# Attention and a gated MLP on one core: a byte-wise step in the weight conversion, and a new order of all operations

## The chip, the cores and the metric

One core of one Trainium2 chip. The metric is device time of one launch in microseconds (us), median of the runs. The five engines that matter are TensorE (PE, matmuls; PEld are its weight loads), VectorE (DVE), ScalarE (ACT), GpSimd (POOL) and SyncE (SP), which issues every DMA of this kernel, one after the other.

## The reference, cut to what matters

```
q, k, v: [4, 8, 768, 64] float32          w_in: [512, 2048], w_out: [2048, 512] float64
k_sum, v_sum = max of k, mean of v over blocks of 32 keys           # 24 each
scores  = [q k^T / 8 where |i - j| < 16,   q k_sum^T / 8 + log 32]
x       = softmax(scores) @ [v, v_sum]     # gathered to [3072, 512]
h       = x @ w_in
out     = (h * cos(h)) @ w_out             # [3072, 512] float32
```

## The kernel before, in words

**Attention.** The 3072 rows of x are eight blocks (0 to 7) of 384 rows, half a batch each. A block has four groups a, b, c, d of two heads. In the tables of the order `a0` is group a of block 0. A group loads q, k and v (`q`, `k`, `v`; 192 KB, 384 KB and about 280 KB by the shapes) and the sums of v (`m`, two DMAs, 72 KB), turns q and k so that the head dimension lies on the partitions (`tq`, `tk` on PE, or `qt`, `kt` on DVE), places them, takes block maxima of k (`ks`), writes the mask into PSUM (`ms`, first eight groups), multiplies (`sc`), copies the scores out (`z`), then maximum (`mx`, DVE), subtraction (`su`, POOL), exponential (`ex`, ACT), sum and inverse (`sm`, `iv`, DVE), normalization (`nm`, POOL), transposition (`tp` on PE with copies `cp`, or `pt`, `po`, `pi`: a 32x32 transpose on DVE and a way through DRAM), the product with v (`va`, PE), and the high and low part of x (`xh`, `xl`).

**Sums of v.** `v0_0` and `v0_1` are the two sums of batch 0 (768 KB each; `l` load, `h` halve, `s` sum). Every later batch has eight parts (`v1_0` to `v1_7`, 192 KB), which share one tile, `kn`: the load of a part waits until the part before is summed.

**Weights.** The float64 weights come as pairs of 32-bit words in 16 slices (`w0` to `w15`, 1 MB each, of a [512, 128] piece of w_in and a [128, 512] piece of w_out). For each slice: `l` load (two DMAs); `ab` (ACT, line 380) takes the absolute value of the high words, 128x1024; `cl` (line 385) clamps them; `sh` (DVE, line 391) shifts left by 3 and masks; `lb` (DVE, line 399) ors in the top three bits of the low words; `fb` (DVE, line 407) ors in the sign and top exponent bit; `hi` and `lo` split the float32 into two fp32r parts. A slice lands in one of six tiles `late`, which are reused: the load of `w5` waits for `fb` of `w1`, `w4` for `w0`, `w8` for `w2`, `w9` for `w3`, `w6` for `w4`.

**MLP.** A step `s` is a block of rows and one slice. `up` (PE, line 706) is 12 matmuls of 384 columns into one PSUM bank; `tu`, `si` (ACT), `re`, `ga` (DVE) make h cos h; `hi`, `lo` split it; `dh` and `dl` (PE, line 757) are 6 and 3 matmuls of 512 columns into three PSUM banks that stay open for the whole run. Steps 0 to 5 are block 0 with slices 0 to 5, steps 6 to 21 block 1 with all slices, steps 22 to 31 block 0 with slices 6 to 15, and then 16 steps for each block. `st` stores a result. Step 0 needs x of all four groups of block 0; step 6 needs all of block 1; step 12 is the first that needs slice 6, step 20 the one for slice 14.

**The order.** `ORDER` is a text of 2118 tokens such as `s4.up.5` (object, operation, PSUM bank or buffer, engine `a`, `v` or `p`). The program walks through it and emits each operation; on every engine the instructions run in just this order, SP's DMAs too, and an instruction that waits holds back all that stand behind it on its engine. The framework adds the semaphores.

Of the kernel before, what the change touches and what calls it, by code (L numbers as in the profile page):

```python
# [32 lines left out]
d0.sc w1.lb a0.nm c0.ex a0.v d0.z.1.a w1.fb.1 a0.tp.0.3 d0.z.0.a a0.tp.1.0 w0.ab.0 a0.m d0.mx w1.hi.a w0.cl.v d0.su
d0.m c0.sm w0.sh.4.5 w5.l w1.lo.p c0.iv w2.ab.0 w0.lb c1.m a0.cp.0.a w2.cl.v c0.nm d0.ex b1.q w0.fb.1 a0.cp.1.a w3.l
a0.va.1 d0.sm w0.hi.a d1.m w2.sh.6.7 w0.lo.p c0.tp.0.2 c1.q d0.iv w5.ab.0 w2.lb b1.tq.3 a1.q a0.xh.a d0.nm c0.tp.1.0
w2.fb.1 c0.cp.0.a d0.v c0.cp.1.a w5.cl.v w2.hi.a c0.va.2 a0.xl w2.lo.p d0.tp.0.6 c0.xh.a w5.sh.4.5 w4.l d0.tp.1.7 a1.m
b0.mx w3.ab.0 a1.tq.0 w5.lb b0.su a1.v a1.cq.a a1.ms.1.0 w5.fb.1 w3.cl.p b0.ex b0.m d0.cp.0.a a1.sc b0.sm b1.cq.a
c1.tq.6 d0.cp.1.a c0.xl a1.z.1.a d0.va.3 b0.iv w3.sh.4.5 b0.nm a1.z.0.a b1.m c1.ms.7.2 d0.xh.a a1.mx c1.cq.a d1.q
w4.ab.0 c1.sc w3.lb a1.su b0.v b0.tp.0.0 w5.hi.a b0.tp.1.1 d0.xl w4.cl.v c1.z.0.a c1.v b0.cp.0.a w4.sh.6.7 c1.z.1.a
b1.ms.3.0 b0.cp.1.a v1_0.l c1.mx a1.ex w8.l w4.lb c1.su b0.va.2 b1.sc a1.sm b0.xh.a w5.lo.p c1.ex d1.tq.1 b0.xl  # L40
b1.z.1.a a2.q a1.iv s0.up.2 w4.fb.0 b1.z.0.a a1.nm w3.fb.1 w4.hi.a a1.tp.0.0 d1.cq.a w4.lo.v w9.l d1.ms.3.6 s0.tu
a1.cp.0.a b1.v c1.sm w8.ab.0 a1.tp.1.7 d1.sc s0.re c1.iv a1.cp.1.a s1.up.4 w8.cl.v c1.nm w10.l s0.si b1.mx d1.v
w8.sh.0.1 w3.hi.a b1.su a1.va.5 d1.z.0.v s1.tu c1.tp.0.7 w8.lb w3.lo.p a2.v d1.z.1.a c1.tp.1.3 a2.tq.6 s1.re c1.cp.1.a
a1.xh.a s2.up.3 d1.mx s1.si c1.cp.0.a s0.ga d1.su w7.l w8.fb.0 s0.hi.a c1.va.2 s0.lo.p w9.ab.1 s1.ga w6.l s3.up.7
w8.hi.v s2.tu b2.q s1.hi.v d1.ex w9.cl.v s1.lo.p a1.xl s0.dh.0.1.4 s2.re w8.lo.p c1.xh.v s3.tu s0.dl c1.xl s2.si s3.re
s4.up.5 a2.cq.v v1_0.s.p d1.sm s3.si s2.ga s1.dh w7.ab.0 d1.iv s2.hi.v d1.nm v1_1.l w9.sh.2.3 s1.dl b1.ex s3.ga
s2.lo.p d1.tp.0.6 w9.lb d1.tp.1.7 s2.dh w7.cl.p s4.tu b1.sm d1.cp.1.a s2.dl d1.cp.0.a s4.re b1.iv s3.hi.a d1.va.7
w9.fb.1 b1.nm s4.si s5.up.6 w7.sh.2.3 s3.lo.p w9.hi.v d1.xh.a s3.dh s4.ga s5.tu w9.lo.p w10.ab.0 d1.xl s5.re s3.dl
w7.lb s4.hi.a b1.tp.0.5 s5.si v1_1.s.p b1.tp.1.7 s4.dh b1.cp.1.a w7.fb.1 b1.cp.0.a s5.ga w7.hi.a b1.va.7 v1_2.l
s4.lo.v w10.cl.v s4.dl s5.hi.a w7.lo.p b1.xh.a s5.dh b1.xl w10.sh.2.3 s6.up.5 v1_2.s.p w6.ab.1 w10.lb s7.up.6 w10.fb.0  # L50
s6.tu s5.lo.p v1_3.l s6.re w12.l w6.cl.v s6.si s5.dl s7.tu w10.hi.v s8.up.7 s7.re w10.lo.p s5.ta.2.a s6.ga s7.si
v1_3.s.v s9.up.2 s5.ta.1.a s7.ga v1_4.l s6.hi.a w6.sh.4.5 s5.st.2 s5.ta.0.a s6.lo.p b2.m s7.hi.a s10.up.3 s8.tu w6.lb
s7.lo.p w12.ab.0 s8.re v1_4.s.p s11.up.6 w6.fb.1 s8.si s9.tu s8.ga v1_5.l w6.hi.a w12.cl.v s6.dh.4.5.7 w11.l s9.re
w6.lo.p w12.sh.0.1 s9.si a2.m s6.dl s8.hi.a s7.dh s5.st.1 s9.ga s8.lo.p s5.st.0 w12.lb s7.dl s8.dh v1_5.s.p s10.tu
s9.hi.a s10.re w12.fb.1 s10.si s8.dl s12.up.2 v1_6.l w11.ab.0 s9.lo.v w15.l s10.ga w12.hi.a w11.cl.v s13.up.3
w11.sh.0.1 s11.tu w12.lo.p s10.hi.a s11.re s9.dh w11.lb s11.si s10.lo.p s11.ga s9.dl w11.fb.1 v1_6.s.p s12.tu s10.dh
w15.ab.0 s12.re w13.l s14.up.6 s11.hi.a w15.cl.v s12.si v1_7.l s11.lo.v b2.v s13.tu s12.ga s10.dl s13.re s12.hi.a
s11.dh w15.sh.0.1 w11.hi.a s12.lo.p w11.lo.p s11.dl s14.tu w15.lb s13.si s12.dh w13.ab.0 s14.re s12.dl v1_7.s.p
w15.fb.1 s15.up.2 s14.si s13.ga s13.hi.a s14.ga a2.k w13.cl.v s13.lo.p s16.up.3 s14.hi.a w15.hi.a w13.sh.0.1 w15.lo.p
s15.tu w13.lb s17.up.6 s15.re w13.fb.0 s15.si s14.lo.p s13.dh s16.tu w14.l s13.dl s16.re s15.ga a2.tk.0.0 s16.si  # L60
a2.tk.1.1 s15.hi.v s14.dh a2.ks.0 s15.lo.p b2.k a2.ck.1.a a2.ks.1 a2.ck.0.a s16.ga s17.tu a2.sc.2.1 w13.hi.a s17.re
s18.up.0 a2.z.1.v w13.lo.p a2.z.0.v b2.qt w14.ab.1 a2.mx s14.dl s17.si w14.cl.v a2.su s15.dh s16.hi.a w14.sh.2.3
s15.dl s17.ga s16.lo.p a2.ex s16.dh w14.lb s16.dl w14.fb.0 s18.tu s19.up.1 s17.hi.a a2.sm w14.hi.a s17.lo.p a2.iv
s18.re s17.dh a2.nm b2.kt.0 s18.si b2.kt.1 w14.lo.p s17.dl b2.ks.0 c2.k a2.tp.0.6 b2.ks.1 b2.sc.2.3 a2.cp.0.a s18.ga
s19.tu a2.tp.1.0 c2.q s20.up.6 b2.z.0.v a2.cp.1.a b2.z.1.v s18.hi.v s19.re s18.lo.p s19.si s21.up.2 s20.tu s20.re
b2.mx s20.si s22.up.0 s19.ga b2.su c2.kt.0 s19.hi.v b2.ex s23.up.3 c2.kt.1 s19.lo.p c2.ks.1 d2.k b2.sm s18.dh s21.tu
s21.re b2.iv s18.dl s21.si c2.qt s19.dh c2.ks.0 d2.q s20.ga s20.hi.v c2.sc.1.6 s20.lo.p s21.ga a2.va.2 s22.tu s21.hi.a
s19.dl d2.kt.0 c2.v s22.re s20.dh s21.lo.p c2.z.0.v a2.xh.v b2.nm s23.tu s20.dl d2.kt.1 s22.si d2.ks.1 s21.dh d2.qt
s23.re a3.q s21.dl s22.ga s23.si s24.up.1 d2.ks.0 s21.ta.1.1.a c2.z.1.v s22.hi.v s21.ta.2.0.v s22.lo.p b2.tp.0.0 c2.mx
b2.tp.1.5 d2.sc.6.7 b2.cp.1.a b2.cp.0.v c2.su s24.tu a2.xl b2.va.5 s24.re s25.up.0 d2.z.0.v b2.xh.a d2.m a3.qt s24.si  # L70
b2.xl c2.ex s21.st.1 d2.z.1.v s26.up.2 c2.m s23.ga s23.hi.v d2.mx s23.lo.p s21.st.2 c2.sm s27.up.6 v2_0.l d2.su s25.tu
c2.iv s24.ga c2.nm s25.re s22.dh.5.7.3 s25.si s22.dl s24.hi.v c2.pt.1 s23.dh s24.lo.p s21.ta.0.0.v c2.po b3.q s26.tu
# [872 lines left out]
```

## Time and profile before

| | |
|---|---|
| median of 3 runs | 661.79 us (661.63 to 662.5) |
| the profiled execution | 663.55 us, of which the span of the profile is 661.8 us |
| busy: PE, DVE, ACT, POOL | 96%, 68%, 46%, 33% of the span |
| chain that ended last, by engine | PE 86%, DMA 4%, SP queue 3%, DVE 3%, POOL 2%, ACT 1% |
| DMA | 72.67 MB, mean 110 GB/s |

Busy PE says little alone, because matmuls are pipelined; the table by stage in the prediction, with idle time, granted clock (PEclk, 1.00 is full speed) and DMA share of each stretch, is the one to read. A row of the timeline has start, duration, engine, line, operation, and in brackets how long the engine sat idle before it and what ended that.

### The profile page before, as it was taken

The numbers are of one execution on the slowest core, as the hardware profiler recorded it, in microseconds if no ns is written. First come the engines' busy times: TensorE is split into PE (matmuls) and PEld (weight loads), VectorE is DVE, ScalarE is ACT, GpSimd is POOL, SyncE is SP. The second block draws the span as 40 slices with busy tenths as digits, with TensorE's granted clock in tenths as the row PEclk, the third lists the DMA queues.
The fourth block names the chain that finished last, engine by engine and source line by source line (L and its number), as shares of the span: only waits on it lengthen the run. The fifth ranks groups of instructions, "written<-read, shape, count | busy, mean of one in ns | idle before, by whom it ended". The sixth has DMA issues, their size and how long they took to land.

```text
span 661.8 us, 13155 instructions
## 1 busy us (share of the span) xinstructions
PE 633.2 (96%) x5141; PEld 560.9 (85%) x5141; DVE 449.9 (68%) x798; ACT 305.8 (46%) x512; POOL 220.7 (33%) x219
## 2 busy tenths in 40 slices
...
GB/s 222 257 271 188 289 16 215 173 113 63 59 125 82 93 120 122 139 58 113 109 104 137 137 96 106 116 43 85 108 169 101 93 94 76 0 1 17 16 17 48
DMA packets 167158, 72.67 MB, mean 110 GB/s; under 512 B 136825, under 2 KB 155833, under 8 KB 167097
## 3 DMA queue, kind: packets, MB, share of 16 engines
...
## 4 chain that ended last, share of the span: by engine, by line
PE 86%; DMA 4%; SPq 3%; DVE 3%; POOL 2%; ACT 1%; issue 1%; DVEq 0%; POOLq 0%; ACTq 0%
PE banks L757 39%; PE banks L706 39%; PE banks L561 4%; PE banks L662 3%; DMA late<-in_moe_w_out_dram 2%; SPq L448 2%; DMA late<-in_moe_w_in_dram 1%; DMA late<-in_q_dram 1%; DVE banks L391 1%; DVE stage L407 1%; POOL stage L385 1%; ACT stage L380 1%; SPq L477 0%; PE banks L548 0%; DVE banks L399 0%
## 5 line engine op out<-in xcount | busy, mean ns | idle before, releaser
L706 PE MATMUL banks<-xh,w 128*128 128x384 f32 x1024 | 272.1, 337 | 0.2 <-ACT pt L342 0.2
L757 PE MATMUL banks<-w,gh 128*128 128x512 f32 x768 | 198.1, 393 | 0.0
L706 PEld LDWEIGHTS banks<-xh,w 128*128 128x128 f32 x1024 | 185.9, 188 | 2.9 <-ACT pt L342 0.4
L706 PE MATMUL banks<-xl,w 128*128 128x384 f32 x512 | 171.4, 335 | 0.0
L757 PEld LDWEIGHTS banks<-w,gh 128*128 128x128 f32 x768 | 142.6, 188 | 28.8 <-ACT gh L342 0.3
L716 ACT ACTIVATE t<-banks 128x384 int32<-128x384 f32 x128 | 62.5, 489 | 164.8 <-DVE gl L348 60.2
L348 POOL TENSOR_TENSOR gl<-t,gh 128x384 fp32r<-128x384 f32 x55 | 56.4, 1026 | 224.0 <-PE banks L757 108.3
L719 DVE SCALAR_TENSOR_TENSOR t<-t,banks 128x384 f32<-128x384 int32 x128 | 69.9, 548 | 67.3 <-ACT t L716 66.4
L757 PE MATMUL banks<-w,gl 128*128 128x512 f32 x384 | 109.8, 394 | 1.0 <-DVE gl L348 1.0
L724 ACT ACTIVATE t<-t 128x384 f32<-128x384 f32 x128 | 66.5, 524 | 75.5 <-DVE t L719 75.1
L706 PEld LDWEIGHTS banks<-xl,w 128*128 128x128 f32 x512 | 96.1, 188 | 1.6
L757 PEld LDWEIGHTS banks<-w,gl 128*128 128x128 f32 x384 | 71.1, 188 | 15.5 <-DVE gl L348 1.1
L585 POOL TENSOR_TENSOR sc<-sc,m 128x720 f32<-128x720 f32 x28 | 40.1, 1431 | 130.3 <-DVE m L580 130.3
L728 DVE TENSOR_TENSOR t<-t,banks 128x384 f32<-128x384 f32 x128 | 69.1, 544 | 13.4 <-ACT t L724 12.4
L609 POOL TENSOR_TENSOR sc<-sc,r 128x720 f32<-128x720 f32 x28 | 39.9, 1426 | 48.9 <-DVE r L606 45.6
L342 ACT CAST gh<-t 128x384 fp32r<-128x384 f32 x68 | 34.7, 511 | 43.9 <-DVE t L728 22.4
L348 DVE TENSOR_TENSOR gl<-t,gh 128x384 fp32r<-128x384 f32 x73 | 41.5, 569 | 18.0 <-PE banks L757 9.8
L344 DVE CAST gh<-t 128x384 fp32r<-128x384 f32 x60 | 23.1, 384 | 28.6 <-PE banks L757 26.8
L348 POOL TENSOR_TENSOR w<-stage,w 128x1024 fp32r<-128x1024 f32 x15 | 36.3, 2418 | 10.4 <-ACT w L342 8.5
L572 DVE SCALAR_TENSOR_TENSOR sc<-banks,mask 128x360 f32<-128x360 f32 x48 | 24.4, 524 | 21.2 <-PE banks L561 21.2
L561 PEld LDWEIGHTS banks<-kd,qd 64*64 64x64 f32 x1344 | 28.4, 135 | 9.2 <-issue 6.6
L662 PEld LDWEIGHTS banks<-pt,vn 120*64 120x64 f32 x624 | 21.0, 141 | 13.0 <-ACT pt L342 7.0
(101 smaller groups left out, 602.1 us busy)
## 6 DMA issues: line engine op xcount, KB each, us to landing
...
```

The lines of the kernel that those rows point to most:

```text
L342: eng.copy(out=out, in_=in_)
L348: eng.tensor_tensor(out=lo, in0=src, in1=hi.bitcast(F32), op=ALU.subtract)
L561: nc.tensor.matmul(out=self.sp[hh][s * QT : (s + 1) * QT, c, lo : lo + n], lhsT=self.qd[rows, t * QT : (t + 1) * QT], rhs=self.kd[rows, ke ...
L585: nc.gpsimd.tensor_tensor(out=self.sc, in0=self.sc, in1=self.m.unsqueeze(2).broadcast_to([P, U, NK]), op=ALU.subtract)
L609: nc.gpsimd.tensor_tensor(out=self.sc, in0=self.sc, in1=self.r.unsqueeze(2).broadcast_to([P, U, NK]), op=ALU.mult)
L662: nc.tensor.matmul(out=self.xps[rows, t * QT : (t + 1) * QT], lhsT=self.vn[:, t, rows], rhs=self.pt[2 * c + hh][s], start=True, stop=True,)
L706: nc.tensor.matmul(out=self.h, lhsT=w_of(name, self.f)[:, c * P : (c + 1) * P], rhs=x_of(self.blk, part, c), start=n == 0, stop=n == last,)
L716: nc.scalar.activation(out=self.t.bitcast(I32), in_=self.h, func=AF.Copy, scale=1.0 / TWO_PI, bias=0.25)
L719: nc.vector.scalar_tensor_tensor(out=self.t, in0=self.t.bitcast(I32), scalar=-TWO_PI, in1=self.h, op0=ALU.mult, op1=ALU.add)
L724: nc.scalar.activation(out=self.t, in_=self.t, func=AF.Sin, scale=-1.0, bias=-0.5 * math.pi)
L728: nc.vector.tensor_tensor(out=self.t, in0=self.t, in1=self.h, op=ALU.mult)
L757: nc.tensor.matmul(out=self.acc[i], lhsT=g[:, i * P : (i + 1) * P], rhs=w_of(name, self.f), start=self.first and n == 0, stop=self.last an ...
```

## The change

**The weight conversion.** `ab` also multiplies by 2^-48 (an argument of the same instruction), and the clamp's bounds are multiplied likewise. `sh` is no longer a shift on DVE: it is an ACT instruction that reads byte 3 of each low word (unsigned 8-bit, every eighth byte), computes byte/32 - 15.5/32 and writes it as an integer, that is, the top three bits of the low word. It depends on the loaded words alone. `lb` now shifts the clamped words left by 3 and ors in these bits, in one DVE instruction; `fb` keeps the sign bit only. DVE has three instructions for a slice instead of four, ACT two instead of one.

```
-    W_LO = struct.unpack("f", struct.pack("I", 896 << 20))[0]
-    W_HI = struct.unpack("f", struct.pack("I", (1151 << 20) - 1))[0]
+    DOWN = 2.0 ** -48
+    W_LO = struct.unpack("f", struct.pack("I", 896 << 20))[0] * DOWN
+    W_HI = struct.unpack("f", struct.pack("I", (1151 << 20) - 1))[0] * DOWN
...
-            nc.scalar.activation(out=self.u.bitcast(F32), in_=self.high.bitcast(F32), func=AF.Abs)
+            nc.scalar.activation(out=self.u.bitcast(F32), in_=self.high.bitcast(F32), func=AF.Abs, scale=DOWN)
...
-        def shift(self, *where):
-            to = self.work_in(where)
-            nc.vector.tensor_scalar(
-                out=to, in0=self.u, scalar1=3, scalar2=0x3FFFFFFF,
-                op0=ALU.logical_shift_left, op1=ALU.bitwise_and,
-            )
-            self.u = to
+        def top_bits(self, *where):
+            self.top = self.work_in(where)
+            byte = self.raw.bitcast(U8).rearrange("p (n b) -> p n b", b=8)[:, :, 3]
+            nc.scalar.activation(out=self.top, in_=byte, func=AF.Copy, scale=1.0 / 32, bias=-15.5 / 32)
...
         def last_bits(self, *where):
-            to = self.work_in(where)
+            to = self.work_in(where) if where else self.top
             nc.vector.scalar_tensor_tensor(
-                out=to, in0=self.low, scalar=29, in1=self.u,
-                op0=ALU.logical_shift_right, op1=ALU.bitwise_or,
+                out=to, in0=self.u, scalar=3, in1=self.top,
+                op0=ALU.logical_shift_left, op1=ALU.bitwise_or,
             )
...
-                out=to, in0=self.high, scalar=-(1 << 30), in1=self.u,
+                out=to, in0=self.high, scalar=-(1 << 31), in1=self.u,
```

**The order.** All of `ORDER` is replaced; the set of operations is the same 2118. PE's matmuls are the same in number and shape. Their order, the PSUM banks, the order of the DMAs and the engine of some operations differ:

| operation | before | after |
|---|---|---|
| low part of a step's product (`lo`) | POOL 55, DVE 73 | POOL 69, DVE 59 |
| parts of the sums of v (`s`) | POOL 12, DVE 14 | POOL 17, DVE 9 |
| clamp of a slice (`cl`) | POOL 2, DVE 14 | POOL 3 (w7, w6, w14), DVE 13 |
| copies out of PSUM (`z`, `ck`, `cq`, `xh`) | ACT 48, DVE 67 | ACT 41, DVE 74 |
| negated results (`ta`) | ACT 14, DVE 10 | ACT 12, DVE 12 |

SP's order up to what step 0 waits for, before and after (`l`, `q`, `k`, `v`, `m` are loads):

```
before: b0.k a0.q a0.k c0.q c0.k d0.k v0_1.l v0_0.l b0.q w1.l d0.q w0.l c0.v c0.m w2.l a0.v a0.m d0.m w5.l c1.m b1.q
        w3.l d1.m c1.q a1.q d0.v w4.l a1.m a1.v b0.m b1.m d1.q b0.v c1.v v1_0.l w8.l a2.q w9.l b1.v w10.l d1.v a2.v
        w7.l w6.l b2.q v1_1.l v1_2.l v1_3.l w12.l
after:  a0.k a0.q d0.k c0.k b0.k b0.q v0_1.l c0.q v0_0.l c0.v w1.l d0.q a0.v w0.l c0.m w2.l a0.m b1.q w5.l d0.m c1.q
        w3.l a1.q d0.v w4.l b0.v d1.q b0.m a1.v w8.l a1.m a2.q w7.l c1.m b1.v c1.v d1.v w9.l b1.m d1.m v1_0.l w10.l
        v1_1.l a2.v w6.l v1_2.l w12.l v1_3.l
```

PE's order around the first steps:

```
before: a0.tp a0.va c0.tp b1.tq c0.tp c0.va d0.tp a1.tq a1.ms a1.sc c1.tq d0.va c1.ms c1.sc b0.tp b1.ms b0.va b1.sc
        d1.tq s0.up a1.tp d1.ms a1.tp d1.sc s1.up a1.va c1.tp a2.tq s2.up c1.va s3.up s0.dh s0.dl s4.up s1.dh
after:  a0.tp c0.tp a0.va c0.va a1.ms b1.tq d0.tp c1.tq a1.tq a1.sc d0.va c1.ms c1.sc b0.tp b1.ms b0.tp b1.sc d1.tq
        b0.va d1.ms d1.sc s0.up s1.up s2.up a1.tp s4.up c1.tp a1.va c1.tp s3.up s0.dh s0.dl s1.dh s1.dl d1.tp
```

PE's order at step 12, after the change: `s6.up s4.dl s7.up s5.dh s5.dl s8.up s6.dh s6.dl s9.up s7.dh s7.dl s10.up s11.up s8.dh s8.dl s9.dh s9.dl s12.up`.

More of the change, by code (lines that the diff above doesn't have):

```diff
@@ L33 @@
[L33 to L72, printed above, removed]
@@ new lines @@
+w9.ab.1 w9.cl.v s2.dh s4.hi.v b1.nm b1.tp.0.0 s2.dl w9.sh.3.4 b1.tp.1.5 d1.m d1.va.7 b1.cp.1.a b1.cp.0.a d1.xh.a s3.dh
+w9.lb w9.fb.1 d1.xl w9.hi.a w7.cl.p v1_0.l v1_0.s.p s5.up.0 a2.tq.7 a2.cq.v w7.sh.3.4 w7.lb b1.va.5 s3.lo.p s4.lo.p
+b1.xh.a s5.tu s3.dl s4.dh b1.xl s6.up.5 s5.re w9.lo.p w7.fb.1 w10.l w10.ab.0 s5.si s5.ga v1_1.l a2.v w6.l v1_1.s.p
+v1_2.l v1_2.s.p w10.cl.v w7.hi.a s5.hi.v s6.tu s6.re s6.si w10.sh.3.4 w7.lo.v s5.lo.v s6.ga w10.lb w10.fb.0 s4.dl
+s7.up.0 s5.dh s5.dl s5.ta.2.v s7.tu s6.hi.a w6.ab.1 s7.re s5.ta.0.a s7.si s8.up.7 s6.lo.p w10.hi.a s5.ta.1.v s7.ga
```

240 lines of the change are left out of this document (138 added, 102 removed).

## The prediction

> **What bounds the kernel now.** I read first the table of windows by stage, for where PE stands still and at what clock.
>
> ```profile
> 0.00:16.50 16.50, 10.85 (x134) 8.32 (x134) 8.27 (x18) 5.41 (x10) 8.24 (x36) 1.00 0.94 222
> 16.50:33.00 16.50, 6.37 (x116) 4.51 (x116) 14.03 (x16) 8.70 (x15) 10.52 (x10) 0.92 0.88 257
> 33.00:50.00 17.00, 12.22 (x119) 9.10 (x120) 14.33 (x17) 9.41 (x16) 14.35 (x8) 0.50 0.93 267
> 50.00:66.00 16.00, 14.31 (x235) 10.79 (x236) 12.60 (x16) 11.40 (x21) 7.22 (x5) 0.97 0.69 188
> 66.00:100.00 34.00, 32.71 (x248) 28.21 (x248) 32.57 (x46) 25.92 (x41) 29.64 (x26) 1.00 0.52 150
> 100.00:150.00 50.00, 50.00 (x300) 45.42 (x300) 44.45 (x62) 31.64 (x53) 34.07 (x34) 1.00 0.54 166
> ...
> 650.00:661.80 11.80, 6.77 (x30) 5.26 (x28) 3.88 (x8) 1.42 (x3) 1.01 (x1) 1.00 0.18 67
> sum 661.80, PE 633.22 PEld 560.95 DVE 449.86 ACT 305.83 POOL 220.68; mean PE 37.25 PEld 33.00 DVE 26.46 ACT 17.99 POOL 12.98
> ```
>
> The columns are stretch, length, busy time of PE, PEld, DVE, ACT and POOL, granted clock, DMA share and GB/s. PE is idle for 661.80 - 633.22 = 28.6 us. The first five rows hold 5.65 + 10.13 + 4.78 + 1.69 + 1.29 = 23.5 of it and the last 5.0, so nothing is left between 100 and 650 us. In the middle PE is the bound at full clock, and the change keeps all its matmuls: there is nothing to win there, only something to lose. What can be won lies ahead of 100 us: idle PE, and the half clock from 33 to 50 us. The last 5 us are the last copies and stores, which both orders do alike; I cost them at nothing.
>
> Next PE's timeline, from the last wait for a load of q to the first steps.
>
> ```profile
> 44.87 0.88 PE L494 MATMUL banks<-ident,late 128*128 128x128 f32 x3 [2.09 <-DMA late<-in_q_dram]
> 45.53 2.61 PE L548 MATMUL banks<-mask,ident 128*128 128x360 f32 x4
> ...
> 57.20 0.92 PE L662 MATMUL banks<-pt,vn 120*64 120x64 f32 x24 [0.82 <-DMA vn<-in_v_dram]
> 58.05 1.09 PE L561 MATMUL banks<-kd,late 64*64 64x96 f32 x48
> ...
> 59.51 0.44 PE L706 MATMUL banks<-xh,w 128*128 128x384 f32 x1
> ...
> 62.73 0.65 PE L618 MATMUL banks<-ident,sc 128*120 128x128 f32 x4 [0.87 <-POOL sc L609]
> 63.22 1.38 PE L548 MATMUL banks<-mask,ident 128*128 128x360 f32 x4
> ```
>
> These rows are a1.tq at 44.87 (it waited for its q), a1.ms, then b0.va at 57.20 (it waited 0.82 for b0's v), b1.sc, the first up of step 0 at 59.51, and d1.ms at 63.22. From 59.51 on PE hardly stops; the start of step 0, and how much attention is already done by then, decide the time.
>
> Why b0's v came so late is told by narrower windows and by SP's timeline.
>
> ```profile
> 41.00:45.00 4.00, 1.91 (x13) 0.50 0.78 184
> 45.00:48.00 3.00, 3.00 (x7) 0.50 0.93 302
> 48.00:51.00 3.00, 3.00 (x58) 0.51 0.82 200
> 51.00:55.00 4.00, 4.00 (x83) 1.00 0.38 89
> ```
>
> ```profile
> 50.59 1.61 SPq L485 DMA_DIRECT2D late<-vs  x2
> 52.31 0.98 SPq L448 DMA_DIRECT2D qn<-in_q_dram  x2
> 53.34 1.25 SPq L469 DMA_DIRECT2D vn<-in_v_dram  x2
> ...
> 80.76 18.91 SPq L246 DMA_DIRECT2D kn<-in_v_dram  x3
> ```
>
> The columns of the windows are here length, PE busy, clock, DMA share, GB/s. Between 51 and 55 us the DMA engines are at 0.38: not volume but SP's order holds b0's v. It is issued at 53.34, behind b1.m (1.61 of SP's time), d1.q and others. The 18.91 us at 80.76 are SP standing at loads of the sums of v, which wait for the one tile kn.
>
> **The change part by part.**
>
> ```profile
> L348 POOL TENSOR_TENSOR w<-stage,w 128x1024 fp32r<-128x1024 f32 x8 | 19.4, 2430 | 3.6 <-ACT w L342 2.9 <-DVE w L344 0.6
> ...
> L380 ACT ACTIVATE stage<-late 128x1024 f32<-128x1024 f32 x11 | 12.6, 1147 | 10.6 <-DMA late<-in_moe_w_out_dram 6.2 <-DVE banks L391 2.3 <-POOL w L348 2.1
> L399 DVE SCALAR_TENSOR_TENSOR banks<-late,banks 128x1024 int32<-128x1024 int32 x10 | 12.2, 1221 | 0.1
> L391 DVE TENSOR_SCALAR banks<-stage 128x1024 int32<-128x1024 int32 x10 | 12.2, 1219 | 1.6 <-POOL stage L385 0.9 <-ACT late L342 0.6
> ...
> L385 DVE TENSOR_SCALAR stage<-stage 128x1024 f32<-128x1024 f32 x9 | 7.8, 870 | 2.4 <-ACT stage L380 2.4
> L342 ACT CAST w<-stage 128x1024 fp32r<-128x1024 f32 x7 | 7.3, 1045 | 3.2 <-DVE stage L407 3.2
> L385 POOL TENSOR_SCALAR stage<-stage 128x1024 f32<-128x1024 f32 x2 | 7.2, 3620 | 0.0
> ```
>
> The rows are those of the first 100 us; the number after the bar is busy time, then mean ns of one.
>
> *Shift.* DVE loses 16 x 1.22 = 19.5 us, 12.2 of it (10 shifts) ahead of 100 us, where it is busy for 81.8 of 100 us. ACT gains 16 byte reads, which the trace does not show: the nearest row is L380, the same 1024 elements at the same eight-byte stride, 1.15 us, so 18.4 us; bounds are 1.05 (the cast, not strided) and twice 1.15 if bytes go slower, so 16.7 to 36.7. ACT is busy for 60.8 of the first 100 us, so it has room. The joins stay at 1.22 each. A slice's chain from `ab` to `fb` is one DVE instruction shorter, 1.2 us, if the byte read isn't behind it in ACT's queue. In itself this moves no load; PE feels it only where a weight is late, and there is no such wait of PE in the trace of before. I count 0 for it, bounded by -1.2 (the first chain) and +1.15 (a byte read ahead of a copy that PE waits for, such as a0.cp, which now stands behind two of them on ACT).
>
> *Shared out anew.* POOL gets 14 low parts, five sums and one clamp more, DVE as much less. [...] Even at twice 0.87 the 13 clamps cost 11 us, less than the 19.5 that DVE loses; I count 0.
>
> *Loads.* Ahead of b0's v SP no longer issues c1.m, d1.m, a1.m, b1.m and a1.v. The four m are 4 x 1.61 = 6.4 us of SP and a1.v at least 1.25, so b0.v goes out about 7.7 us earlier, near 45.6, and d1.q (0.98) and b0.m (1.61) behind it, done by 49.7; some 2 us to land gives 52. By volume: from a1.q, which landed at 44.87, to b0.m there are w4, d0.v, b0.v, d1.q and b0.m, by the shapes 1.9 MB, at the 267 GB/s of the third row 7.1 us, so 52.0. Both say 52 where it was 57.2. After that the new order has b0.va (0.92), d1.ms (1.38) and d1.sc (1.09), so by the loads step 0 can start at 55.3.
>
> *PE.* From a1.tq to step 0 it was 59.51 - 44.87 = 14.6 us, 0.8 of it waiting. The new order has a1.ms and c1.tq done before a1.tq (2.61 + 0.88 at half clock; 1.75 at full) and takes d1.ms and d1.sc into this stretch, 2.47. If the clock is as it was, the half-clock stretch after a1.tq is as long as before and other matmuls fall into it: 14.6 - 0.8 - 1.75 + 2.47 = 14.5. a1.q goes out with c1.m and d1.m no longer ahead, 3.2 us earlier by SP's time, 0.6 by volume (0.15 MB less ahead of it): a1.tq at 41.7 to 44.3, and I take 42.7, nearer the volume, as the DMA share stood at 0.93 up to 50 us. Step 0 then starts at 57.2, bounds 55.3 and 58.8.
>
> *Sum.* Step 0 starts 2.3 us earlier (59.5 - 57.2), and d1.ms and d1.sc, 2.5, are already done then: -4.8. Behind it the stalls of before (0.87 here and the 1.29 of the fifth row, 2.2 in all) meet a new order that puts a1.tp two ups later; a1.va then waits on ACT's copies, which stand behind w3's cast and w8's byte read, and s3.up on w3's low part. I leave these at 2.2 and add 0.5 for single waits in the middle, where some ups stand closer ahead of their downs. Net -4.3: the profiled execution, 663.55, would be 659.25. It stands 1.76 above the median, and I take the gain over unchanged: 661.79 - 4.3 = 657.5.
>
> **The rivals.**
>
> *The clock stays up, and DVE's relief takes the stalls (15%).* The clock fell to 0.50 in the third row, after the row with 10.13 us of idle PE. If the new order breaks this up, the 14.5 us lose about 2.9 (half of the six us up to 51, where the fourth narrow window shows 1.00 again); step 0 is then held by the loads, 55.3, and without half of the stalls it is -1.9 more and -1.1: 654.5. [...] Against it: a0.va still waits for a0's m, whose place in volume is unchanged, and for copies that now stand behind w0's `ab` and byte read.
>
> *Given back in the queues (13%).* The early loads only move other loads behind: a1.m now stands 1.4 MB behind b0.m (a1.v, w8.l and itself), 5.3 us at 267 GB/s, c1.m further still, and a1.va and c1.va wait for them; or s3.up waits for w3, whose `fb` stands behind step 0's `re` on DVE. Then -4.3 shrinks to zero: 661.8. For: PE has only some 10 us from step 0 to s3.up. Against: a1.m would land near 57.3, and a1.va comes about nine us after step 0's start.
>
> *Slower: slice 6 is late at s12.up (12%).* Before, w6.l stood ahead of v1_1.l on SP. Now v1_1.l is ahead of it and waits for v1_0's sum on POOL, which stands behind two normalizations and w7's clamp of 3.62; the row with 18.91 shows how SP stands at such loads. Slice 6 has its clamp on POOL as well: `ab` 1.15, clamp 3.62, two joins 2.44, cast 1.05, over 8.3 us without low part and queues, and its low part stands behind those of steps 7 and 9. What PE has to do between s6.up and s12.up follows from these rows of the chain of waits:
>
> ```profile
> 640.26 6.26 PE banks L706 x36
> 646.52 10.26 PE banks L757 x45
> ```
>
> An up is 6.26 / 3 = 2.09 and a down matmul 0.228: five ups and 48 down matmuls, 21.4 us. From s6's low part, which comes after s6's chain of some 4 us, to slice 6's low part POOL has that clamp of 3.62, two low parts of slices at 2.43, three of steps (384 of 1024 columns, 0.9 each) and a sum of v, about 2: some 13 us, an estimate. The margin is then about 4 us. Each us beyond it is a us of the kernel: 7.5 beyond the margin make 3.2 us slower than before, 665. In the trace PE never waits for weights, which speaks against it.
>
> **How the numbers follow.** The forecast has 55%, and its own range from the bounds of step 0's start (58.8 to 55.3) and 1 to 2 us of stalls is 655 to 660.5. The three rivals have 15, 13 and 12%, and 5% I can't name. The range for eight in ten takes in the first two rivals and leaves out the slower one: 653 to 662.5. About 0.2%, 1.3 us, can be told from no change here: faster means below 660.5, slower above 663.1. Faster is the forecast, the first rival and a little of the rest, 0.72; same 0.14; slower 0.14.
>
> **What would show it.** Right: step 0's first up between 55 and 59, with d1.ms and d1.sc ahead of it; b0.va near 53 without a long wait for v; no L391; about 16 ACT reads of bytes near 1.15; PE 50 of 50 in the windows from 100 us on. Wrong: a wait of PE for a weight at s12.up or s20.up; step 0 after 59.5; a window in the middle with PE below its length; a byte read of over 2 us.

## The result, and the profile after

| | before | after |
|---|---|---|
| median, measured side by side | 662.14 us (661.63 to 663.6, 4 runs) | 658.69 us (658.02 to 659.73, 4 runs) |
| ratio, 95% interval | 1 | 0.994 (0.9923 to 0.9958) |
| the profiled execution, its span | 663.55 us, 661.8 us | 658.99 us, 657.2 us |
| step 0's first up starts | 59.51 us | 55.81 us |
| last matmul ends | 656.77 us | 652.17 us |
| busy: DVE, ACT, POOL | 449.9, 305.8, 220.7 us | 437.0, 316.7, 247.4 us |

The changed kernel is faster by 3.45 us (medians) or 4.6 us (profiled executions); the forecast was 4.3. In the code after the change most line numbers are lower by one: up is L705, down L756, the byte read L394, the join L398, `fb` L406. In the experiments below they are a few higher: `va`, L661 here, is L664 or L665 there, and L671 in kernels 8 and 9.

The windows by stage of the kernel after (columns as in the prediction):

```profile
16.50:33.00 16.50, 11.33 (x167) 8.30 (x167) 15.82 (x20) 10.47 (x17) 13.08 (x11) 0.80 1.08 289
33.00:50.00 17.00, 13.61 (x196) 10.76 (x197) 15.99 (x23) 15.88 (x25) 12.63 (x8) 0.70 0.90 247
50.00:66.00 16.00, 16.00 (x214) 14.28 (x212) 14.06 (x20) 13.96 (x22) 13.62 (x9) 1.00 0.80 219
66.00:100.00 34.00, 33.97 (x239) 29.57 (x234) 31.28 (x51) 27.08 (x42) 25.96 (x23) 1.00 0.55 173
100.00:150.00 50.00, 48.95 (x293) 43.96 (x291) 41.44 (x60) 29.72 (x47) 30.61 (x27) 1.00 0.53 144
```

Idle PE in the first two rows here is 5.17 and 3.39 us, where before it was 10.13 and 4.78. From 50 to 100 us PE no longer stands still. Instead it loses 1.05 us between 100 and 150, where it lost nothing before. DVE is busy for all but 0.7 and 1.0 us of the first two rows, ACT for all but 1.1 of the second: the new order leaves neither of them room in the head.

PE's timeline after, from d0's scores to step 0, and the longest of the three waits behind it:

```profile
26.88 2.44 PE L560 MATMUL banks<-kd,late 64*64 64x96 f32 x48 [2.27 <-ACT late L499]
...
37.36 1.55 PE L661 MATMUL banks<-pt,x 120*64 120x64 f32 x24 [2.46 <-ACT pt L344]
...
43.33 0.83 PE L493 MATMUL banks<-ident,late 128*128 128x128 f32 x6
...
52.54 0.92 PE L661 MATMUL banks<-pt,vn 120*64 120x64 f32 x24
53.38 1.48 PE L547 MATMUL banks<-mask,ident 128*128 128x360 f32 x4
54.79 1.09 PE L560 MATMUL banks<-kd,late 64*64 64x96 f32 x48
55.81 0.45 PE L705 MATMUL banks<-xh,w 128*128 128x384 f32 x1
...
129.25 0.45 PE L705 MATMUL banks<-xh,w 128*128 128x384 f32 x1 [1.05 <-DVE stage L406]
```

These are d0.sc, c0.va, then in one row the three matmuls of c1.tq and the three of a1.tq, then b0.va (no wait for v any more), d1.ms, d1.sc and step 0. The row at 37.36 waits for c0's copies: on ACT they stand behind w2's `ab` and byte read, the last of them behind a cast of w0 too. The row at 129.25 is s17.up, whose PSUM bank 5 still holds the converted bits of w13 until its `fb`.

SP's timeline after, at b0's v, and then the groups by shape of the first 100 us:

```profile
42.05 0.97 SPq L468 DMA_DIRECT2D vn<-in_v_dram  x2
...
44.66 2.27 SPq L484 DMA_DIRECT2D vn<-vs  x2
```

```profile
L398 DVE SCALAR_TENSOR_TENSOR banks<-stage,banks 128x1024 int32<-128x1024 int32 x11 | 13.5, 1226 | 2.5 <-ACT banks L394 2.0
...
L394 ACT ACTIVATE banks<-late 128x1024 int32<-128x1024 uint8 x11 | 12.3, 1118 | 0.3 <-DVE r L605 0.3
...
L387 DVE TENSOR_SCALAR stage<-stage 128x1024 f32<-128x1024 f32 x9 | 6.6, 731 | 1.1 <-ACT stage L382 1.1
```

b0.v goes out at 42.05 instead of 53.34. The joins (L398) kept their 1.22 us and waited 2.0 us for byte reads; a byte read takes 1.12 us (1.15 was taken); DVE's clamps (L387) take 0.73 us in the mean, where they took 0.87.

### The profile page after: what moved, and what is told of

The parts are those of the page before. It is cut to its first block, busy times and chain, and to the rows that moved or that the text cites. A ratio compares the mean times of both kernels' runs of the same rounds, so it can differ in the third digit from the quotient of the medians.

```text
span 657.2 us, 13183 instructions
## 1 busy us (share of the span) xinstructions
PE 635.1 (97%) x5141; PEld 562.7 (86%) x5141; DVE 437.0 (67%) x768; ACT 316.7 (48%) x520; POOL 247.4 (38%) x251
## 4 chain that ended last, share of the span: by engine, by line
PE 88%; DVE 4%; DMA 4%; ACT 1%; SPq 1%; issue 1%; POOL 0%; ACTq 0%; DVEq 0%; POOLq 0%
PE banks L756 38%; PE banks L705 38%; PE banks L560 4%; PE banks L661 4%; PE banks L547 2%; DMA late<-in_moe_w_out_dram 1%; PE banks L617 1%; DMA out_dram<-stage 1%; PE banks L506 1%; DMA late<-in_k_dram 1%; DMA kn<-in_v_dram 1%; SPq L484 0%; DVE t L727 0%; DVE gl L350 0%; PE banks L493 0%
## 5 line engine op out<-in xcount | busy, mean ns | idle before, releaser
L705 PE MATMUL banks<-xh,w 128*128 128x384 f32 x1024 | 278.1, 338 | 1.1 <-DVE stage L406 1.1
L756 PE MATMUL banks<-w,gh 128*128 128x512 f32 x768 | 198.7, 394 | 0.5 <-DVE t L727 0.5
L705 PEld LDWEIGHTS banks<-xh,w 128*128 128x128 f32 x1024 | 186.6, 188 | 6.1 <-DVE stage L406 1.7
L705 PE MATMUL banks<-xl,w 128*128 128x384 f32 x512 | 171.7, 335 | 0.0
L756 PEld LDWEIGHTS banks<-w,gh 128*128 128x128 f32 x768 | 142.5, 188 | 29.0 <-DVE t L727 0.8
L350 POOL TENSOR_TENSOR gl<-t,gh 128x384 fp32r<-128x384 f32 x69 | 70.9, 1031 | 226.5 <-ACT gh L344 99.2
L756 PE MATMUL banks<-w,gl 128*128 128x512 f32 x384 | 110.1, 394 | 0.0
L705 PEld LDWEIGHTS banks<-xl,w 128*128 128x128 f32 x512 | 96.1, 188 | 2.8
L756 PEld LDWEIGHTS banks<-w,gl 128*128 128x128 f32 x384 | 70.9, 188 | 12.8
L350 DVE TENSOR_TENSOR gl<-t,gh 128x384 fp32r<-128x384 f32 x59 | 38.5, 656 | 16.3 <-ACT gh L344 12.0
L350 POOL TENSOR_TENSOR w<-stage,w 128x1024 fp32r<-128x1024 f32 x14 | 34.6, 2471 | 12.0 <-ACT w L344 7.0
L253 POOL TENSOR_TENSOR kn<-kn 96x256 f32<-96x256 f32 (+1 forms) x32 | 20.0, 625 | 32.1 <-DMA kn<-in_v_dram 16.4
L560 PE MATMUL banks<-kd,qd 64*64 64x24 f32 (+1 forms) x1344 | 30.9, 231 | 0.8 <-ACT qd L499 0.6
L600 DVE TENSOR_REDUCE r<-sc 128x6 f32<-128x726 f32 x28 | 25.2, 899 | 8.0 <-ACT sc L597 7.9
```

The lines of the kernel that those rows point to most:

```text
L350: eng.tensor_tensor(out=lo, in0=src, in1=hi.bitcast(F32), op=ALU.subtract)
L560: nc.tensor.matmul(out=self.sp[hh][s * QT : (s + 1) * QT, c, lo : lo + n], lhsT=self.qd[rows, t * QT : (t + 1) * QT], rhs=self.kd[rows, ke ...
L705: nc.tensor.matmul(out=self.h, lhsT=w_of(name, self.f)[:, c * P : (c + 1) * P], rhs=x_of(self.blk, part, c), start=n == 0, stop=n == last,)
L756: nc.tensor.matmul(out=self.acc[i], lhsT=g[:, i * P : (i + 1) * P], rhs=w_of(name, self.f), start=self.first and n == 0, stop=self.last an ...
```

## The experiments

In each kernel below all operations are there, unless the text says otherwise. "Half clock" is worked out from windows of 2 us between 8 and 64 us: twice the sum of (1 - granted clock) x 2 us. "Without waits" is the time from step 0's first up to the end of the last matmul, less PE's waits of over 0.15 us in it (the column ahead of it). Times are in us; each ratio is to runs of the kernel before on the same chip, whose medians lay between 662.1 and 662.9.

| kernel | first up | half clock | waits behind it | without waits | median | ratio to before, 95% interval |
|---|---|---|---|---|---|---|
| before | 59.51 | 20.4 | 2.0 | 595.2 | 662.14 | 1 |
| after | 55.81 | 17.0 | 1.8 | 594.6 | 658.69 | 0.994 (0.9923 to 0.9958) |
| 1 byte step, old order | 61.20 | 17.0 | 3.2 | 596.3 | 665.92 | 1.0052 (1.0038 to 1.0066) |
| 2 shift, new order | 62.61 | 30.6 | 7.8 | 595.9 | 673.06 | 1.0158 (1.0145 to 1.0172) |
| 3 old, five loads later | 55.70 | 13.6 | 4.5 | 595.3 | 664.43 | 1.0021 (1.0008 to 1.0035) |
| 4 new, those loads earlier | 62.27 | 23.8 | 2.1 | 594.5 | 665.93 | 1.0045 (1.0032 to 1.0059) |
| 5 copies first | 57.95 | 17.0 | 1.6 | 594.5 | 663.03 | 1.0003 (0.9987 to 1.0019) |
| 6 s17.up later | 56.93 | 20.4 | 0.7 | 594.6 | 658.35 | 0.9931 (0.9916 to 0.9946) |
| 7 both | 59.01 | 20.4 | 0.5 | 594.2 | 660.64 | 0.9971 (0.9956 to 0.9985) |
| 8 matmuls added, 21 | 62.70 | 6.8 | 1.6 | 594.0 | 663.46 | 1.0014 (0.9999 to 1.0028) |
| 9 matmuls added, 5 | 54.78 | 6.8 | 0.5 | 594.3 | 656.59 | 0.9915 (0.9896 to 0.9934) |
| 10 byte reads early, old order | 60.71 | 17.0 | 4.2 | 595.9 | 668.09 | 1.0091 (1.007 to 1.0111) |
| 11 the same, loads later | 63.29 | 27.4 | 4.5 | 597.2 | 669.29 | 1.0113 (1.0089 to 1.0138) |
| 12 s0.up ahead of d1 | 56.75 | 20.5 | 3.1 | 596.8 | 663.61 | 1.0011 (0.9995 to 1.0027) |

All columns but the last two are of one profiled execution, and they don't always say the same as the median: the wait for a q near 16 us, and with it the start of the half clock, changes from one execution to the next. Kernel 6 shows by how much. Its edit acts only behind 100 us, and yet that wait was 1.41 us where it was 0.78 in the kernel after, the half clock was 3.4 us longer, and step 0 began 1.1 us later. Kernels 3 and 5 were profiled in a favourable execution, the second shortest of twelve in both (662.31 and 660.84 us): the clock granted over the span was 0.988 and 0.986 in these, and 0.980 to 0.987 and 0.978 to 0.985 in the others.

**1 and 2: each half of the change alone.**

Kernel 1 is the old order with the new conversion; kernel 2 the new order with DVE's shift, where the shift of eight slices had to go behind their clamp:

```
1:  the ORDER of before, the code of after
2:  the code of before, the ORDER of after, with, for w0 w2 w3 w4 w5 w6 w8 w15:
-   w2.ab.0 w2.sh.0.1 ... w2.cl.v w2.lb
+   w2.ab.0 ... w2.cl.v w2.sh.0.1 w2.lb
```

> The kernel before with its old order, but with the new conversion (ScalarE's byte read in place of VectorE's shift, the shift inside the join). Order theory (the gain comes from what stands ahead of b0.v on SP and from d1.ms and d1.sc ahead of step 0): b0.v is still issued near 53.3 and step 0's first up stays within 0.7 us of 59.5, so the time is 0 to -1 us against before, ratio 0.9985 to 1.000. Relief theory (VectorE, busy 82 of the first 100 us, was what held PE back, and 1.2 us less for each slice brings the gain): step 0 starts 2 us or more earlier and the time falls by about 3 us, ratio 0.9955.

> The new order with the old conversion: VectorE's shift and the join as before; in eight slices the shift is put right behind the clamp, where the byte read stood ahead of it. Order theory: step 0 starts at 55.8 to 57, time within 1.5 us of the changed kernel, 658.5 to 660 where before is 662. Relief theory: VectorE has 19.5 us more to do than in the changed kernel and holds PE back again, time near before, 661 to 663.

Both theories fail in both: the byte step alone costs 0.5%, the new order alone, with the shifts at these places, 1.6%, and the two together gain 0.6%. Kernel 1's table of ACT's waits between 24 and 60 us says why the byte step is not free there; the row of before is the second:

```profile
ACT stage L385 <- DVE banks L401: 5.1, 4, 1.3
```

```profile
ACT stage L380 <- DVE banks L391: 2.3, 1, 2.3
```

The byte reads stand where the shifts stood, behind the clamp. Now the join waits for ACT's byte read, and ACT's next `ab` waits for the join, because both slices use the same work tile: four times about 1.3 us, a round trip between two queues where DVE alone did it before. PE gets it through c0's copies (the row at 40.77 is c0.va, which did not wait in the kernel before) and through b0's low part:

```profile
32.94 1.66 PE L664 MATMUL banks<-pt,vn 120*64 120x64 f32 x24 [5.98 <-ACT pt L347]
34.53 1.11 PE L620 MATMUL banks<-ident,late 128*120 128x128 f32 x4
38.05 0.87 PE L496 MATMUL banks<-ident,late 128*128 128x128 f32 x3 [2.42 <-DMA late<-in_q_dram]
...
40.77 1.55 PE L664 MATMUL banks<-pt,x 120*64 120x64 f32 x24 [1.43 <-ACT pt L347]
...
61.20 0.45 PE L708 MATMUL banks<-xh,w 128*128 128x384 f32 x1 [0.93 <-DVE xl L353]
```

In kernel 2 it is DVE that is full. Its windows:

```profile
33.00:50.00 17.00, 11.24 (x89) 8.59 (x90) 16.37 (x21) 10.95 (x18) 13.10 (x8) 0.50 0.99 274
50.00:66.00 16.00, 15.84 (x276) 12.98 (x269) 15.69 (x20) 10.01 (x19) 9.04 (x5) 0.89 0.60 176
```

DVE is busy for 32.1 of these 33 us (30.1 in the kernel after, which is further on), ACT for 21.0 (29.8). The new order puts copies and high parts of the head on DVE in the place of the shifts; with the shifts still there PE waits, the clock stays at half for 30.6 us, and 7.8 us of waits follow behind step 0.

**3 and 4: the loads ahead of b0.v.**

```
3, SP:  before  ... d0.v w4.l a1.m a1.v b0.m b1.m d1.q b0.v c1.v ...
        edited  ... d0.v w4.l b0.m d1.q b0.v a1.v a1.m c1.m b1.m d1.m c1.v ...
4, SP:  after   ... d0.v w4.l b0.v d1.q b0.m a1.v w8.l a1.m ...
        edited  w5.l c1.m ... w3.l d1.m ... d0.v w4.l a1.m a1.v b0.m b1.m d1.q b0.v w8.l ...
```

> The kernel before, only that the loads c1.m, d1.m, a1.m, b1.m and a1.v are issued behind b0.v (five tokens moved in the order; all else as it was). Loads theory (SP's order holds b0.v and so step 0): b0.v is issued 4 to 8 us earlier, b0.va does not wait for v, step 0's first up comes 1 to 3 us earlier, time -1 to -3 us against before, ratio 0.9955 to 0.9985. PE theory (the half clock and PE's own work ahead of step 0 set its start): b0.va's wait of 0.8 goes, step 0 is at most 0.8 us earlier, ratio 0.9985 to 1.000; above that if a1.va or b1's softmax now waits for its late m.

> The changed kernel, only that c1.m, d1.m, a1.m, a1.v, b1.m, and with them b0.m and d1.q, are issued ahead of b0.v again as in the kernel before. Loads theory: b0.v is issued near 53 again, b0.va waits, step 0's first up comes at 58 to 59.5 where the changed kernel has 55.8, time +2.5 to +4 us against the changed kernel, ratio to before 0.998 to 1.001. PE theory: step 0 within 1 us of 55.8, time at most 1 us over the changed kernel, ratio 0.9945 to 0.9965.

In the profiled executions the loads theory holds for the start of step 0: 3.8 us earlier in the old order, 6.5 us later in the new one. Kernel 4's wait is the old one, a b0.va that waits for v:

```profile
59.00 0.92 PE L664 MATMUL banks<-pt,vn 120*64 120x64 f32 x24 [1.52 <-DMA vn<-in_v_dram]
```

It explains 1.5 of the 6.5 us. The larger part is the clock and the waits that keep it down: 23.8 us at half instead of 17.0, as PE waits once more for a q and for copies between 24 and 48 us. This is no matter of one execution: the six of kernel 4 were granted a clock of 0.979 to 0.983 over the span, the four of the kernel after 0.985 to 0.987. In kernel 3's profiled execution it went the other way, 13.6 us instead of 20.4. But kernel 3 is not faster in the end, and its timeline shows what came in place:

```profile
55.70 0.45 PE L709 MATMUL banks<-xh,w 128*128 128x384 f32 x1 [1.32 <-DVE xl L351]
```

```profile
65.60 0.45 PE L665 MATMUL banks<-pt,late 120*64 120x64 f32 x8 [0.67 <-ACT pt L345]
...
68.45 0.43 PE L621 MATMUL banks<-ident,late 128*120 128x128 f32 x2 [1.81 <-DVE late L347]
```

Step 0 now waits for DVE, and the two groups behind it (a1 and c1) wait for ACT and DVE: 4.5 us of waits instead of 2.0. Behind these two stands a load, but not one of those that were moved. SP issues w8's load at 57.2 us, at 57.3 in the kernel before, and ACT now stands for it 3.92 us instead of 0.80, with a1's copy and DVE's next clamp behind it; ACT's row of kernel 3, and then that of before:

```profile
64.15 1.14 ACT L383 ACTIVATE stage<-late 128x1024 f32<-128x1024 f32 x1 [3.92 <-DMA late<-in_moe_w_out_dram]
```

```profile
64.86 1.16 ACT L380 ACTIVATE stage<-late 128x1024 f32<-128x1024 f32 x1 [0.80 <-DMA late<-in_moe_w_out_dram]
```

So of the 3.8 us at step 0 1.2 are left at the last matmul (655.54 instead of 656.77), and nothing in the median, which this execution does not stand for. This is the forecast's second rival, in the old order, with w8 as the late load instead of a1's and c1's m. The new order has w8's load ahead of a1.m; there it goes out at 49.8 us.

**5, 6 and 7: the two waits that the change brought.**

```
5, ACT:  - w0.ab w0.sh ... a0.cp.1 a0.cp.0      - w2.ab w2.sh c0.cp.1 ... c0.cp.0
         + w0.ab a0.cp.1 a0.cp.0 w0.sh          + c0.cp.1 c0.cp.0 w2.ab w2.sh
6, PE:   - s15.up s13.dh s16.up s13.dl s17.up.5 s18.up.6 s14.dh s14.dl
         + s15.up s13.dh s16.up s13.dl s14.dh s17.up.5 s18.up.6 s14.dl
7:       both
```

> The changed kernel, only that on ScalarE the copies c0.cp stand ahead of w2's two steps (ab and the byte read) and a0.cp right behind w0.ab. Queue theory (c0.va waits 2.46 us for c0.cp, which stands behind w2.ab and the byte read on ScalarE): c0.va starts at 34.5 to 35.5 where it was 37.36, and step 0 comes 1 to 2 us earlier, ratio to the changed kernel 0.997 to 0.9985, about 657. Load theory (what follows c0.va waits for loads of q and v in any case): c0.va is earlier, but the gap moves to a1.tq or b0.va and step 0 stays within 0.5 us of 55.8, ratio to the changed kernel 0.9995 to 1.0005.

> The changed kernel, only that s17.up and s18.up stand behind s14's six high down matmuls on TensorE, so that the up which needs PSUM bank 5 comes some 4 us of other matmuls later. Bank theory (the 1.05 us of idle TensorE at 129.2 us is the wait for bank 5, held by w13's bits): that gap is gone and the time falls by 1.0 to 1.2 us, about 657.5. Rival (what stands behind s17.up is late itself, so that the wait comes back at the next matmul): the sum of gaps stays at 1.8 and the time within 0.3 us.

> Both edits together, the copies first and the later s17.up. If queue theory and bank theory both hold the gains add up: 2 to 3 us under the changed kernel, 656 to 657; if only the bank theory holds, 1.0 to 1.2 under it, 657.5.

The bank theory holds: in kernel 6 the wait at 129 us is gone, the waits behind step 0 fall from 1.8 to 0.7 us, and the stretch from step 0 to the last matmul from 596.36 to 595.26 us. The medians show little of it, 0.3 us, and the two ratios' intervals overlap; in the profiled execution step 0 began 1.1 us later than in that of the kernel after, for the reason given above.

The copies first were a mistake, and neither theory had the reason. Kernel 5's timeline:

```profile
36.14 1.55 PE L664 MATMUL banks<-pt,x 120*64 120x64 f32 x24 [1.00 <-ACT pt L347]
37.61 2.35 PE L550 MATMUL banks<-mask,ident 128*128 128x360 f32 x4
42.84 0.90 PE L496 MATMUL banks<-ident,late 128*128 128x128 f32 x3 [2.88 <-DVE stage L409]
```

c0.va is 1.2 us earlier, as wanted. But w2's conversion is later by the same copies, it holds PSUM banks 0 and 1 from the byte read to `fb`, and b1.tq needs bank 0: it waits 2.88 us for that `fb` (L409). The wait for ACT has for the most part become a wait for a bank. While PE waits there, the clock, which was at full from 39.4 us on, falls to half for another 3.4 us. The profiled execution is 1.9 us longer than that of the kernel after, the median 4.3; what the rest is, no trace shows, but the other executions of kernel 5 were granted a lower clock, as said above. Kernel 7 has both effects, a b1.tq that waits 2.70 us and no wait at 129 us; with 660.64 us neither of its two forecasts came.

**8 and 9: the clock.**

```
+        def warm(self, i, n):
+            for _ in range(n):
+                nc.tensor.matmul(out=bank(i)[:, : QC * NK]..., lhsT=ident, rhs=mask[:, 0:QC, :], start=True, stop=True)
8: d0.wm.1.4 d0.sc    a0.wm.0.3 a0.tp    c0.wm.4.3 c0.tp    a0.wm.2.3 a0.va    c0.wm.3.8 c0.va
9: a0.wm.0.2 a0.tp    c0.wm.3.3 c0.va    (and s17.up later, as in 6)
```

> The changed kernel with 21 matmuls more that nothing reads (128x360 of the mask, 0.345 us each at full clock by the mask rows, 7.2 us in all), put where TensorE waits: four ahead of d0.sc, three each ahead of a0.tp, c0.tp and a0.va, eight ahead of c0.va. Clock theory (the 17 us at half clock come from TensorE's idle time between 24 and 37 us, and cost what TensorE does in them twice its time): the granted clock stays at 1.00 or falls for less than 6 us, from c0.va on the matmuls run at full speed and step 0 comes 2 to 3.5 us earlier, 655 to 657 in all. Rival (the loads set the head, or the clock falls whatever TensorE does): step 0 within 0.7 us of 55.8, or later by part of the 7.2 us, 658.5 to 662.

> The kernel with the later s17.up, and five mask matmuls more that nothing reads: two ahead of a0.tp, three ahead of c0.va. Each costs two of the profile's 128x360 matmuls, 0.69 us at full clock (the 21 of the run before were so 14.5 us and not 7.2), together 3.5 us, the three ahead of c0.va inside its wait of 2.1 to 2.5 us. Clock theory (a stretch of some four us without idle TensorE brings the full clock back, as in the run before, and what follows c0.va then takes half the time): full clock from about 34 us on, step 0 at 53 to 55.5 us, time 1 to 3 us under the kernel with the later s17.up alone, 655.5 to 657.5. Rival (the copies and loads, not the clock, set the head): c0.va no earlier than 37, step 0 at 55.5 to 58, time equal or up to 2 us more.

Kernel 8's timeline shows its added matmuls:

```profile
27.67 4.02 PE L556 MATMUL banks<-mask,ident 128*128 128x360 f32 x8 [2.14 <-ACT sc L347]
...
40.74 5.11 PE L556 MATMUL banks<-mask,ident 128*128 128x360 f32 x16
45.77 0.92 PE L671 MATMUL banks<-pt,x 120*64 120x64 f32 x24
```

Each counts as two rows, so they were twice as long as planned. The clock did nearly what the theory said (half for 6.8 us, less than 6 expected, 17.0 in the kernel after), but the added work itself put c0.va at 45.77. So kernel 8 shows the half clock shrink as PE's waits are filled, from 17.0 to 6.8 us, and nothing about what this is worth. Kernel 9, with five, shows that. Its windows and its timeline:

```profile
16.50:33.00 16.50, 11.64 (x171) 8.24 (x170) 15.83 (x21) 10.30 (x17) 13.52 (x11) 0.79 1.04 290
33.00:50.00 17.00, 14.24 (x207) 9.81 (x207) 16.22 (x22) 16.28 (x25) 12.73 (x8) 1.00 0.96 254
```

```profile
34.63 2.08 PE L556 MATMUL banks<-mask,ident 128*128 128x360 f32 x6
37.24 0.92 PE L671 MATMUL banks<-pt,x 120*64 120x64 f32 x24 [0.53 <-ACT pt L347]
...
40.57 0.55 PE L496 MATMUL banks<-ident,late 128*128 128x128 f32 x3 [1.00 <-DVE stage L409]
```

From 33 us on the clock is full (0.70 in the kernel after). c0.va still starts at 37.2, since ACT's copies set that, but it takes 0.92 us where it took 1.55, and so on, until b1.tq meets the bank of w2 again (1.00 at 40.57). Step 0 starts at 54.78. All six executions were granted a clock of 0.992 to 0.995 over the span (0.985 to 0.987 in the kernel after). With 656.59 us (655.86 to 657.63, 6 runs) this kernel is ahead of both: 1.8 us under kernel 6, 2.1 under the kernel after, whose shortest run was 658.02. The intervals of the ratios still overlap, from 0.9923 to 0.9934 with that of the kernel after and from 0.9916 to 0.9934 with that of kernel 6.

**10 and 11: the byte reads early in the old order.**

```
10:  - w2.ab.0 w0.lb ... w2.cl.v ... w2.sh.6.7
     + w2.ab.0 w2.sh.6.7 w0.lb ... w2.cl.v ...      (so for all slices; w3 and w10 ahead of cl)
11:  the same, and SP's order as in 3
```

> The old order with the new conversion, as in the first run, but each byte read stands right behind its own ab on ScalarE (ahead of the clamp for w3 and w10), not where VectorE's shift stood. Place theory (the first run lost 3.4 us because ab of the next slice, copies and VectorE's join wait across the two queues when the byte read stands behind the clamp): the waits of ab for the join (5.1 us between 24 and 60 us) go, step 0 comes back to 58.5 to 60, time 661 to 663, 3 us under the first run. Room theory (ScalarE has no room for the byte reads in the old order wherever they stand): time stays near 666, step 0 near 61.

> The same, and c1.m, d1.m, a1.m, b1.m and a1.v behind b0.v. If the gain of the change is the loads plus a byte read in its right place, this has most of it: step 0 at 54.5 to 56.5, VectorE's two waits of 1.3 us ahead of step 0 (seen with the loads alone) shorter, time 658 to 661. If the rest of the new order is what makes the loads pay (what moved behind b0.v is then late in the old one): stalls behind step 0 of 4 us as with the loads alone, time 662 to 665.

In these two the byte reads of w4, w6, w7, w9 and w13 land in PSUM banks whose former content is still to be read, so a mask of c1, s2's and s6's products, c1's x and parts of w9 and w15 are replaced: the two kernels compute something else, and only their times are of use. That also adds waits that belong to the banks, and one of them is large:

```profile
53.83 1.09 PE L563 MATMUL banks<-kd,qd 64*64 64x96 f32 x48 [2.78 <-ACT banks L397]
```

This is c1.sc, which waits for w4's byte read in its bank. At a1.sc kernel 10 was ahead of kernel 1 (46.01 instead of 47.60), though a0.va had come 2.0 us later and `ab` still waited 4.4 us for joins. Kernel 11 has the same reads and, with the later loads, 27.4 us at half clock. The runs do not tell the two theories apart; what they show is that an early byte read needs two free PSUM banks, and that the old order has none to give at this place. A version with banks of its own was not tried.

**12: what d1.ms and d1.sc do ahead of step 0.**

```
PE:  - b0.va d1.ms d1.sc s0.up s1.up
     + b0.va s0.up d1.ms d1.sc s1.up
```

> The changed kernel, only that on TensorE s0.up stands ahead of d1.ms and d1.sc instead of behind them. Cover theory (the high and low part of b0's x end 1.9 us after b0.va, and d1.ms and d1.sc fill just this wait): s0.up starts near 55.3, only 0.5 us earlier than in the changed kernel, after 1.5 to 2 us of idle TensorE ahead of it, and the time is 1.5 to 2 us longer, 660 to 661. Account theory (the forecast's: work done ahead of step 0 and step 0's start count alike, so their order is of no consequence): s0.up starts 2.3 to 2.5 us earlier, near 53.4, time within 0.5 us of the changed kernel, 658.2 to 659.2.

The cover theory holds for the wait of 1.5 to 2 us, and the price is higher than it said (4.4 us in the profiled execution, 4.9 in the median):

```profile
54.12 0.92 PE L664 MATMUL banks<-pt,vn 120*64 120x64 f32 x24
56.75 0.44 PE L708 MATMUL banks<-xh,w 128*128 128x384 f32 x1 [1.71 <-DVE stage L409]
```

b0.va is 1.6 us later than in the kernel after (the clock fell earlier in this execution); from there on the edit shows: 1.71 us of idle PE ahead of s0.up, and 3.1 us of waits behind it instead of 1.8.

## Why the prediction was right, and where it was not

The time came out as forecast (658.99 for the profiled execution, 659.25 forecast; the median 658.69, 657.5 forecast), but out of other terms. By the last matmul the kernel gained 4.60 us:

| term | forecast | measured | from |
|---|---|---|---|
| start of step 0 | -2.3 | -3.70 | 59.51, 55.81 |
| d1.ms and d1.sc done ahead of it | -2.5 | -2.4 | 53.38 to 55.81 |
| waits behind step 0 | +0.5 | -0.25 | 2.03, 1.78 |
| pace behind step 0 | none | +1.8 | 595.23 to 594.58 is -0.65, where -2.4 was due |

The terms beyond the forecast cancel: step 0 gave 1.4 us more and the waits 0.75 more, and the pace, which no term had, took 1.8. That the sum is right to 0.3 us is luck. The start of step 0 is also one execution's: in kernel 6, the same up to there, it was 56.93, close to the 57.2 of the forecast.

**Start of step 0: an earlier a1.tq, as forecast, but the larger part is the clock.** a1.tq came at about 43.7 (the second half of the row at 43.33) instead of 44.87: 1.2 us, where 2.2 were forecast. The other 2.5 us lie between a1.tq and step 0, which took 12.1 us and not 14.5. The failed step is "if the clock is as it was, the half-clock stretch after a1.tq is as long as before": the full clock came back at 43.3 us, ahead of a1.tq, and not 6.0 us behind it (44.87 to 50.9 before). Windows as long as one step of the clock (last section) show why, first before, then after:

```profile
40.69:44.11 3.42, 2.08 (x18) 1.56 (x15) 3.32 (x5) 1.79 (x3) 3.04 (x2) 0.50 0.81 196
44.11:47.52 3.41, 2.65 (x7) 1.66 (x7) 1.53 (x2) 1.86 (x5) 3.41 (x2) 0.50 0.88 253
47.52:50.93 3.41, 3.41 (x57) 2.48 (x57) 2.19 (x5) 1.39 (x4) 2.24 (x2) 0.50 0.87 237
```

```profile
36.51:39.92 3.41, 2.56 (x26) 2.18 (x27) 3.16 (x6) 3.41 (x5) 3.21 (x3) 0.50 0.95 304
39.92:43.34 3.42, 3.42 (x13) 2.48 (x13) 3.42 (x5) 2.69 (x5) 2.60 (x2) 0.50 0.92 227
```

In both kernels the clock came back at the end of the first window in which PE was busy throughout. Before, a1.tq's wait of 2.09 us for its q lies across the first two windows; after, a1.tq waits for no load. By these windows the earlier q did more than bring a1.tq forward: the wait for it was also what kept the clock down, and the forecast had it in the first role only. Kernel 4 agrees: there a1.tq waits 0.92 us for its q again, in a window with 1.91 us of busy PE, and the clock falls to half for another 3.4 us. The loads were not the bound of 55.3 that the forecast used, either: b0.v went out at 42.05, and b0.va waited for nothing.

**The byte step at nothing was wrong, in both directions.** It costs 0.5% where the order is not made for it (kernel 1), and the new order without it costs 1.6% (kernel 2). The forecast looked for the weights that PE waits for, and there were none, before or after. What counts is that the byte read takes ACT's time and, where it is put early, two PSUM banks, and that the new order spends again what DVE saves: in the first 100 us, where 12.2 us of shifts have gone, DVE is busy for 85.0 us instead of 81.8. Over the whole run it is busy for 12.9 us less. So what failed here is the assumption that the parts can be priced one by one and added up.

**The stalls.** The three waits of before are gone (0.87, 0.18, 0.98). In their place are 1.05 for bank 5, 0.50 and 0.23 further on. The forecast had 2.7 us in all (2.2 left and 0.5 new), the trace has 1.78, and at none of the places that it named. One of its signs of being wrong, a window in the middle with PE below its length, did come (48.95 of 50 us).

**The pace** was not in the forecast. All kernels in the old order but the disturbed 11 need 595.2 to 596.3 us without waits, all in the new one from 594.0 to 594.6 (kernel 2, 595.9, is the exception; kernel 12 has d1.ms and d1.sc in it), though these have 2.4 us less to do. The median from one down matmul to the next is 227 ns in the kernels before, 1 and 3, and 229 in after, 2, 4, 5, 6 and 7, so it goes with PE's order. That order changes more often between up and down (81 times from up to down, 45 before). Whether this is the cause stays open.

**The rivals.** The clock: half true. It did not stay up, but came back 7.6 us sooner; kernel 9, with the full clock from 33 us on and the later s17.up, came to 656.59, half of the way from 658.69 to that rival's 654.5. Given back in the queues: not in the changed kernel, but in kernel 3, by w8's load. Slice 6: s12.up and s20.up waited for nothing; POOL's estimated margin of 4 us was enough. The work shared out anew, counted at 0: no run shows the bound of clamps that take twice as long, the author's estimate. What the runs show is a mean that fell from 0.87 to 0.73 us in the first 100 us, but POOL was hardly busier there (71.0 us instead of 70.0), so that tests the bound little; over the whole run, with POOL busy for 27 us more, the mean went from 0.82 to 0.79. A single clamp of 1.42 us at 120.94 stands in w15's chain ahead of the wait for bank 5, and what share of that wait it has was not tested.
